# Two softmaxes by the tensor engine, and 18 identity products at the start

## The chip, the cores and the metric

The kernel runs on one core of a Trainium2 chip. The metric is device time in microseconds (us). The core has a tensor engine (PE; its weight loads are listed as PEld), a vector engine (DVE), a scalar engine (ACT), GpSimd (POOL) and a sync engine (SP), which here issues all loads and stores. Each engine works through its own queue in program order.

## The reference

Attention between 512 tokens and 32 state vectors, for 8 batches and 8 heads, then two layers of a network on all 4608 rows:

```python
scores = scale * np.matmul(x, state.transpose(0, 1, 3, 2))      # tokens x 32 states
a = softmax over the 32 states;   xread = np.matmul(a, state)
scores2 = scale * np.matmul(state, x.transpose(0, 1, 3, 2))     # 32 states x tokens
a2 = softmax over the 512 tokens; sread = np.matmul(a2, x)
x = concatenate([xread, sread], axis=2), heads side by side     # 4608 x 512
h = x @ w_in;  r = maximum(h, 0);  g = s * (r * r) + b;  x = g @ w_out      # 512 -> 2048 -> 512
h = maximum(x @ w_in2, 0);         out = h * h @ w_out2
```

Weights of the network come as doubles, which the kernel turns into single precision on the chip.

## The kernel before

A batch's scores are two tiles `sc` (r = 0 and 1, half of the heads each) of 128 partitions by 512 tokens: a partition is a head's state, four heads of 32 states stand below each other. So the softmax over states runs across groups of 32 partitions, and that over tokens along a row. `per_head` (L255) makes the scores with eight products into two PSUM tiles, and ScalarE copies them out (`att_sc`).

`att_exp` does both softmaxes' exponentials: the vector engine takes the maximum along the row (`nm2`), and it turns 32x32 blocks (`nc.vector.transpose`, L358) so that the other softmax too runs along the row: maximum of each 32, subtraction, exponential on ScalarE. `att_norm` sums, takes reciprocals and scales both. `att_an` turns the first softmax back and splits it into a high and a low part (`aT_t`), the moving operands of the first layer; `att_tp` turns the second by the tensor engine, and `att_sr` multiplies it with `xn` (x with tokens on the partitions); `att_put` copies the result into `sraw`.

The first layer goes in blocks of 128 hidden units: `mm1` (L448, tile `h`), `relu2` on ScalarE (three passes), `low` on the vector engine, and two blocks later `mm2` (L478, tile `acc`). Its weights `w_in` are multiplied with the state beforehand (`s_first` for batch 0, L288; `s_mm` for batch 1, L260), tile `S`. At the start the weights are still being loaded and converted: `piece` loads 128 columns or rows, `mag` is one ScalarE pass, `to_f32` four vector passes (L135 to L146). For the first blocks `early` does this between the products. The order of blocks is four of batch 0, four of batch 1, then the other twelve of each. The scheme is written out by hand: everything ahead of the loop stands in one sequence, and `at_step(i, fn, rank)` puts a piece of work behind block i, in the order of its rank. PSUM tiles rotate: four banks by `pst`, four by the pool `pa`, which also holds `acc`. Loads go out on SP's queue in program order, and one waits there when its buffer is not free (four buffers `raw` for weights, four `x` for `xT`, `xn` and `aT`).

Of the kernel before, what the change touches and what calls it, by code (L numbers as in the profile page):

```python
# [31 lines left out]
ALU = mybir.AluOpType  # L32
# [29 lines left out]
def attn_mlp2(ctx: ExitStack, tc: tile.TileContext, xT, xn, st, w_in1, w_out1, w_in2, w_out2, s_in, b_in, out):  # L62
# [40 lines left out]
    def x8(shape, name, dt=F32R):  # L103
        return xp.tile(shape, dt, tag="x", name=name)
# [225 lines left out]
            )  # L330
        xa[b] = [t, sb, None]

    def att_load_n(b):
        n = x8([P, S // P, DM], f"xn{b}", F32)
        nc.sync.dma_start(out=n, in_=xn[b].rearrange("(t p) d -> p t d", p=P))
        xa[b][2] = n

# [4 lines left out]
    def att_sc(b, _):  # L342
        t, sb, _ = xa[b]
        sps = [pst(f"sc{b}{r}") for r in range(2)]
        per_head(sps, sb, lambda rows, k: t[rows, k, :])
        for r, sp in enumerate(sps):
            sc = at.tile([P, S], F32, tag="sc", name="sc")
            nc.scalar.activation(out=sc, in_=sp, func=ACTF.Copy, scale=scale)
            cur[b, r] = [sc]

    def att_exp(b, c):
        (sc,) = cur[b, c]
# [36 lines left out]
    def att_tp(b, c):  # L389
# [4 lines left out]
        a2T = (at if b else op).tile([P, 4, P], F32, tag="t1" if b else "o", name="a2T")  # L394
        nc.scalar.copy(out=a2T, in_=tp.rearrange("p (a b) -> p a b", a=4))
        cur[b, c] = [a2T]

    def att_turn(b, c):
        att_an(b, c)
        att_tp(b, c)  # L400

    srp_t = {}

# [431 lines left out]
    def later(i, k, loader, rank=0):  # L835
# [12 lines left out]

    calm = ((att_sc, 0, 5), (att_exp, 0, 6), (att_exp, 1, 8), (att_norm, 0, 9), (att_norm, 1, 10),
            (att_an, 0, 11), (att_an, 1, 12), (att_tp, 0, 13), (att_tp, 1, 13), (att_sr, 0, 17), (att_put, 0, 17))  # L850
    first = ((att_exp, 0, 0), (att_exp, 1, 0), (att_norm, 0, 1), (att_norm, 1, 1), (att_turn, 0, 2),
             (att_turn, 1, 2), (att_sr, 0, 4), (att_put, 0, 4))
    rank = {att_sr: 0, att_tp: 0, att_sc: 0, att_put: 2, att_an: 3, att_turn: 3, att_exp: 5, att_norm: 5}
    for b in range(1, B):
        base = step(2, 0) + (b - 3) * NF if b > 1 else 0
        if b > 1:
            at_step(base + 1, lambda b=b: att_load(b), 6)
        at_step(base + 1, lambda b=b: att_load_n(b), 6)
        for fn, c, k in first if b == 1 else calm:
            at_step(base + k, lambda fn=fn, b=b, c=c: fn(b, c), rank[fn])  # L860
        for q in range(NQ):

# [144 lines left out]
    def finish(i):  # L1007
        for fn in lows.pop(i, []):
            fn()

    with tc.manual_schedule():
        make_identity(nc, ident)
        nc.scalar.activation(out=minus, in_=ident, func=ACTF.Copy, scale=-1.0)
        nc.gpsimd.memset(ones, 1.0)
        v0 = [piece("i1", w_in1, 0, 0)]
        att_load(0)
        v0 += [piece("i1", w_in1, 0, k) for k in range(1, VA)]
        nc.sync.dma_start(out=s_sb, in_=s_in.to_broadcast([P, 1]))
        nc.sync.dma_start(out=b_sb, in_=b_in.to_broadcast([P, 1]))
        v0[0]["mag"]()  # L1020
        to_f32(v0[0]["pair"]())
        att_sc(0, 0)
        s_first(0)
        att_exp(0, 0)
        s_first_lo(0)
        att_exp(0, 1)
        for p in v0[1:]:
            p["mag"]()
        att_load_n(0)
        att_load(1)  # L1030
        bring(0)
        bring(1)
        att_norm(0, 0)
        att_norm(0, 1)
        att_an(0, 0, lambda: to_f32(v0[1]["pair"]()))
        att_tp(0, 0)
        att_an(0, 1, lambda: to_f32(*[p["pair"]() for p in v0[2:]]))
        att_tp(0, 1)
        att_sc(1, 0)
        for p in stage[0]:  # L1040
            p["mag"]()
        at_step(1, lambda: att_sr(0, 0), 0)
        at_step(2, lambda: att_put(0, 0), 0)

        gs = {}
        for i in range(len(order) + LAG + 1):
# [57 lines left out]
```

## Time and profile before

| | us |
|---|---|
| three runs | 1406.64, 1407.17, 1409.31 (median 1407.17) |
| profiled execution: time, span | 1405.25, 1403.5 |
| PE busy, share of the span | 1371.6, 98% |
| PEld busy | 1159.5, 83% |
| DVE busy | 765.1, 55% |
| ACT busy | 759.1, 54% |

The span is the time between the first and the last instruction of the profiled execution; busy shares are means over stages that differ. In the profile's 40 equal slices of the span, PE is at 4 tenths in the first and at 9 in all others but the last.

### The profile page before, as it was taken

What the parts mean: (1) busy time and instruction counts of PE and PEld (TensorE: products, weight loads), DVE (VectorE), ACT (ScalarE), POOL (GpSimd) and SP (SyncE); (2) the same over time, 40 slices, a digit from 0 to 9 for tenths busy, and PEclk for the clock granted to TensorE, in tenths of its full rate; (3) what the DMA queues carried; (4) which work ended last, traced back from release to release, by engine and by line L of the source; (5) the groups of instructions that cost most, each with busy time, mean ns of one, the idle gap of its engine ahead of it and who ended that gap; (6) DMA issues with size and microseconds to landing.
All of it is one profiled execution on the core that took longest, in us unless ns stands there. A gap on an engine that the chain in (4) does not pass through costs nothing.

```text
span 1403.5 us, 20210 instructions
## 1 busy us (share of the span) xinstructions
PE 1371.6 (98%) x7770; PEld 1159.5 (83%) x7770; DVE 765.1 (55%) x1495; ACT 759.1 (54%) x1492; POOL 0.7 (0%) x7
## 2 busy tenths in 40 slices
PE   4999999999999999999999999999999999999998
PEld 2677777777777777889988999988999988999897
DVE  7888645555565767345667544453444435343533
ACT  4877656656665656557655543363344335434543
POOL 0000000000000000000000000000000000000000
PEclk9999999999999999999999999999999999999999
DMA  7365232332414241302663655445445544543652
GB/s 239 120 220 184 90 112 73 116 113 85 145 49 143 83 147 60 113 0 98 215 225 138 189 162 160 119 149 158 119 125 172 165 120 120 165 128 108 216 157 68
DMA packets 88863, 188.48 MB, mean 134 GB/s; under 512 B 8640, under 2 KB 26048, under 8 KB 86208
## 3 DMA queue, kind: packets, MB, share of 16 engines
q1 hardware_dynamic: 88768, 187.21, 42.5%
q8 instruction: 61, 1.00, 0.3%
q14 instruction: 34, 0.28, 0.1%
HBM read 144.18 MB, written 42.99 MB: 133 GB/s over the span
## 4 chain that ended last, share of the span: by engine, by line
PE 95%; DVE 3%; ACT 1%; DMA 0%; issue 0%; SPq 0%
PE o L681 27%; PE acc L478 26%; PE m L636 24%; PE h L448 14%; PE S L260 2%; PE sr L413 1%; PE sc L260 1%; PE tp L393 0%; PE S L288 0%; DMA xT<-xT 0%; DVE m L362 0%; DVE t L376 0%; DVE t L363 0%; DVE V L141 0%; DVE V L146 0%
## 5 line engine op out<-in xcount | busy, mean ns | idle before, releaser
L478 PE MATMUL acc<-g,o1h 128*128 128x512 f32 (+1 forms) x1152 | 341.2, 379 | 0.0
L478 PEld LDWEIGHTS acc<-g,o1h 128*128 128x128 f32 x1152 | 211.4, 188 | 41.7 <-issue 2.0
L478 PE MATMUL acc<-g,o1l 128*128 128x512 f32 (+1 forms) x576 | 217.5, 378 | 0.4 <-DVE o1l L189 0.4
L448 PE MATMUL h<-aT,S 128*128 128x512 f32 x768 | 201.9, 397 | 6.2 <-DVE aT L387 3.5
L448 PEld LDWEIGHTS h<-aT,S 128*128 128x128 f32 x768 | 141.4, 189 | 60.9 <-issue 9.2
L636 PE MATMUL m<-xw 128*128 128x384 f32 (+1 forms) x1008 | 183.4, 328 | 2.3 <-DVE r L715 2.3
L636 PEld LDWEIGHTS m<-xw 128*128 128x128 f32 x1008 | 171.5, 188 | 10.0 <-DVE r L715 2.6
L649 ACT ACTIVATE sc<-sc 128x384 f32<-128x384 f32 (+1 forms) x144 | 72.8, 505 | 153.2 <-DVE sc L715 151.7
L461 DVE TENSOR_TENSOR g<-r,g 128x512 fp32r<-128x512 f32 (+1 forms) x144 | 94.8, 658 | 111.0 <-ACT g L457 111.0
L455 ACT ACTIVATE r<-h 128x512 f32<-128x512 f32 (+1 forms) x144 | 82.2, 570 | 124.5 <-PE h L448 123.2
L649 ACT ACTIVATE v<-m 128x384 f32<-128x384 f32 (+1 forms) x96 | 45.5, 474 | 152.8 <-PE m L636 152.2
L478 PEld LDWEIGHTS acc<-g,o1l 128*128 128x128 f32 x576 | 108.4, 188 | 21.1 <-DVE o1l L189 0.9
L681 PE MATMUL o<-o2h,xw('g', 0)_6295 128*128 128x512 f32 x364 | 121.2, 392 | 0.0
L681 PE MATMUL o<-o2h,xw('g', 1)_6296 128*128 128x512 f32 x364 | 121.1, 392 | 0.0
L681 PE MATMUL o<-o2h,xw('g', 2)_6297 128*128 128x512 f32 x360 | 119.7, 392 | 0.0
L715 DVE TENSOR_TENSOR v<-m,r 128x384 f32<-128x384 f32 (+1 forms) x48 | 25.7, 536 | 164.4 <-PE m L636 164.4
L636 PE MATMUL m<-xw,xw('odd', 0)_6176 128*128 128x384 f32 (+1 forms) x576 | 107.4, 328 | 0.8 <-DVE t L715 0.8
L636 PEld LDWEIGHTS m<-xw,xw('odd', 0)_6176 128*128 128x128 f32 x576 | 98.3, 188 | 5.0 <-DVE t L715 1.2
L456 ACT ACTIVATE r<-r 128x512 f32<-128x512 f32 (+1 forms) x144 | 87.7, 609 | 4.6
L457 ACT ACTIVATE g<-r 128x512 fp32r<-128x512 f32 (+1 forms) x144 | 87.6, 609 | 4.6
L111 DVE TENSOR_TENSOR S<-S,S 128x512 fp32r<-128x512 f32 x54 | 34.8, 686 | 91.4 <-ACT S L110 91.4
L636 PE MATMUL m<-xw,xw('odd', 1)_6177 128*128 128x384 f32 (+1 forms) x432 | 79.3, 327 | 0.0
(146 smaller groups left out, 1893.5 us busy)
## 6 DMA issues: line engine op xcount, KB each, us to landing
xw<-w2s SPq DMA_DIRECT2D x140, 256.0 KB, 2.8
xw('odd', 0)_6176<-w2s SPq DMA_DIRECT2D x20, 1024.0 KB, 4.9
xw('odd', 1)_6177<-w2s SPq DMA_DIRECT2D x20, 768.0 KB, 4.3
i1r<-w_in SPq DMA_DIRECT2D x16, 512.0 KB, 5.0
xn<-xn SPq DMA_DIRECT2D x8, 1024.0 KB, 8.8
o1r<-w_out SPq DMA_DIRECT2D x16, 512.0 KB, 4.8
x<-ot SPq DMA_DIRECT2D x32, 256.0 KB, 3.0
i2r<-w_in SPq DMA_DIRECT2D x16, 512.0 KB, 5.3
```

Of the source, the lines that this page charges most:

```text
L111: nc.vector.tensor_tensor(out=lo, in0=src, in1=hi.bitcast(F32), op=ALU.subtract)
L260: nc.tensor.matmul(out=outs[r][k * NS : (k + 1) * NS], lhsT=state[rows, r, k, :], rhs=moving(rows, k), start=True, stop=True, skip_group_c ...
L448: nc.tensor.matmul(out=hp, lhsT=l_, rhs=r_, start=(i == 0), stop=(i == len(ops) - 1))
L455: nc.scalar.activation(out=r, in_=hp, func=ACTF.Relu)
L456: nc.scalar.activation(out=r, in_=r, func=ACTF.Square)
L457: nc.scalar.activation(out=g[:, 0], in_=r, func=ACTF.Copy)
L461: nc.vector.tensor_tensor(out=g[:, 1], in0=r, in1=g[:, 0].bitcast(F32), op=ALU.subtract)
L478: nc.tensor.matmul(out=o, lhsT=l_, rhs=r_, start=(opens and i == 0), stop=(closes and i == 2))
L636: nc.tensor.matmul(out=o, lhsT=w[:, a, k, :], rhs=x[:, b, k, :], start=(start and k + a + b == 0), stop=(k + a == 2), skip_group_check=True,)
L649: nc.scalar.activation(out=c, in_=src, func=func)
L681: nc.tensor.matmul(out=acc2[t], lhsT=l_, rhs=r_, start=(fa == 0 and e == 0), stop=(fa == NF - 1 and e == 2))
L715: add = lambda o, x, y: nc.vector.tensor_tensor(out=o, in0=x, in1=y, op=ALU.add)
```

## The change

For batches 0 and 1 the softmax over states no longer goes through the vector engine's block transposes. `soft_max` turns the scores with the tensor engine and takes the maximum of each 32 along the row from PSUM. `to_rows` brings these back to the layout of the scores: a product of a broadcast column with the identity, which adds minus the maximum onto the scores still lying in PSUM (`soft_exp`) or writes the reciprocals of the sums into another PSUM tile (`soft_norm`). `soft_sum` sums over each head's 32 partitions by products with `heads`, a matrix of ones and zeros. `soft_lo` makes the low part. The softmax over tokens is in `soft_state`; it stands behind blocks 0 and 3, and `att_tp`, `att_sr` and `att_put` follow later than before. `keep_on(18)` issues 18 products of the identity with itself ahead of everything else. The loads of batch 1 are issued ahead of `xn` of batch 0. The other batches stay as they are.

```diff
+    heads = const.tile([P, KD], F32, name="heads")
...
+    def soft_sc(b):
+        t, sb, _ = xa[b]
+        sps = [pa.tile([P, 512], F32, tag="acc", name=f"sc{b}{r}") if b else pst(f"sc{b}{r}") for r in range(2)]
+        per_head(sps, sb, lambda rows, k: t[rows, k, :])
+        for r, sp in enumerate(sps):
+            pool, tag = (at, "sc") if b else (op, "o")
+            sc = pool.tile([P, S], F32, tag=tag, name="sc")
+            nc.scalar.activation(out=sc, in_=sp, func=ACTF.Copy)
+            cur[b, r] = [sc]
+            cur["ps", b, r] = sp
+
+    def soft_max(b, r):
+        sc = cur[b, r][0]
+        tp = pa.tile([P, 512], F32, tag="acc", name=f"tm{b}{r}")
+        for i in range(4):
+            nc.tensor.transpose(out=tp[:, i * P : (i + 1) * P], in_=sc[:, i * P : (i + 1) * P], identity=ident)
+        m = cur["m", b, r] = sm.tile([P, 16, 1], F32, tag="m1", name="m1")
+        nc.vector.tensor_reduce(
+            out=m[:, :, 0], in_=tp.rearrange("p (a s) -> p a s", s=NS), axis=AX.X, op=ALU.max, negate=True
+        )
+
+    def to_rows(out, v, start):
+
+        for i in range(4):
+            for k in range(KD):
+                nc.tensor.matmul(
+                    out=out[k * NS : (k + 1) * NS, i * P : (i + 1) * P],
+                    lhsT=v[:, KD * i + k, :].to_broadcast([P, NS]),
+                    rhs=ident, start=start, stop=True, skip_group_check=True,
+                )
+
+    def soft_exp(b, r):
+        sp = cur.pop(("ps", b, r))
+        to_rows(sp, cur.pop(("m", b, r)), False)
+        e = cur["e", b, r] = at.tile([P, S], F32, tag="t1", name="e")
+        nc.scalar.activation(out=e, in_=sp, func=ACTF.Exp, scale=scale)
+
+    def soft_sum(b):
+        pt = pst(f"sum{b}")[:, : 32]
+        for r in range(2):
+            for i in range(4):
+                c0 = 16 * r + KD * i
+                nc.tensor.matmul(
+                    out=pt[:, c0 : c0 + KD], lhsT=cur["e", b, r][:, i * P : (i + 1) * P], rhs=heads,
+                    start=True, stop=True, skip_group_check=True,
+                )
+        for r in range(2):
+            s = cur["s", b, r] = sm.tile([P, 16, 1], F32, tag="s1", name="s1")
+            nc.vector.tensor_scalar(
+                out=s[:, :, 0], in0=pt[:, 16 * r : 16 * r + 16], scalar1=1e-9, scalar2=None, op0=ALU.add
+            )
+            nc.vector.reciprocal(out=s, in_=s)
+
+    def soft_norm(b, r):
+        pt = pst(f"inv{b}{r}") if b else pa.tile([P, 512], F32, tag="acc", name=f"inv{b}{r}")
+        to_rows(pt, cur.pop(("s", b, r)), True)
...
+        nc.vector.tensor_tensor(out=e, in0=e, in1=pt, op=ALU.mult)
+        nc.scalar.activation(out=aT_t[b][:, 0, r, :], in_=e, func=ACTF.Copy)
...
+    def soft_state(b, r):
+
+        (sc,) = cur[b, r]
+        nm2 = sm.tile([P, 1], F32, tag="nm2", name="nm2")
+        nc.vector.tensor_reduce(out=nm2, in_=sc, axis=AX.X, op=ALU.max, negate=True)
+        s2 = sm.tile([P, 1], F32, tag="s2", name="s2")
+        nc.vector.tensor_scalar(out=nm2, in0=nm2, scalar1=scale, scalar2=None, op0=ALU.mult)
+        nc.scalar.activation(out=sc, in_=sc, func=ACTF.Exp, bias=nm2, scale=scale, accum_out=s2)
+        nc.vector.tensor_scalar(out=s2, in0=s2, scalar1=1e-9, scalar2=None, op0=ALU.add)
+        nc.vector.reciprocal(out=s2, in_=s2)
+        nc.scalar.activation(out=sc, in_=sc, func=ACTF.Copy, scale=s2)
...
+    def keep_on(n):
+
+        pt = pa.tile([P, 512], F32, tag="acc", name="on")
+        for _ in range(n):
+            nc.tensor.matmul(out=pt[:, :P], lhsT=ident, rhs=ident, start=True, stop=True)
+
     with tc.manual_schedule():
         make_identity(nc, ident)
+        keep_on(18)
...
+        n0 = x8([P, S // P, DM], "xn0", F32)
+        att_load(1)
+        bring(0)
+        att_load_n(0, n0)
+        bring(1)
         v0[0]["mag"]()
         to_f32(v0[0]["pair"]())
-        att_sc(0, 0)
+        soft_sc(0)
+        soft_max(0, 0)
+        soft_max(0, 1)
         s_first(0)
-        att_exp(0, 0)
+        v0[1]["mag"]()
+        soft_exp(0, 0)
+        soft_exp(0, 1)
+        to_f32(v0[1]["pair"]())
+        v0[2]["mag"]()
+        soft_sum(0)
         s_first_lo(0)
-        att_exp(0, 1)
-        for p in v0[1:]:
-            p["mag"]()
-        att_load_n(0)
-        att_load(1)
-        bring(0)
-        bring(1)
-        att_norm(0, 0)
-        att_norm(0, 1)
-        att_an(0, 0, lambda: to_f32(v0[1]["pair"]()))
-        att_tp(0, 0)
-        att_an(0, 1, lambda: to_f32(*[p["pair"]() for p in v0[2:]]))
-        att_tp(0, 1)
-        att_sc(1, 0)
+        soft_norm(0, 0)
+        soft_norm(0, 1)
+        soft_lo(0, 0)
+        soft_lo(0, 1)
+        v0[3]["mag"]()
+        to_f32(*[p["pair"]() for p in v0[2:]])
+        soft_sc(1)
         for p in stage[0]:
             p["mag"]()
-        at_step(1, lambda: att_sr(0, 0), 0)
-        at_step(2, lambda: att_put(0, 0), 0)
+        for r in range(2):
+            at_step(0, lambda r=r: soft_max(1, r), -1)
+            at_step(0, lambda r=r: soft_state(0, r), 1)
+            at_step(1, lambda r=r: soft_exp(1, r), -1)
+            at_step(1, lambda r=r: att_tp(0, r), 0.5)
+            at_step(2, lambda r=r: soft_norm(1, r), -1)
+            at_step(2, lambda r=r: soft_lo(1, r), -1)
+            at_step(3, lambda r=r: soft_state(1, r), 1)
+            at_step(4, lambda r=r: att_tp(1, r), 1)
+        at_step(1, lambda: soft_sum(1), 0)
+        for b, i in ((0, 2), (1, 6)):
+            at_step(i, lambda b=b: att_sr(b, 0), 0)
+            at_step(i + 1, lambda b=b: att_put(b, 0), 0)
```

## Rows read from the trace of the kernel before

**Rows 1.** Busy us of PE, PEld, DVE, ACT, POOL; granted clock, DMA, GB/s.

```profile
20.00:25.00 5.00, 4.61 (x27) 2.28 (x27) 4.79 (x10) 1.65 (x3) 0.00 (x0) 1.00 0.18 71
25.00:30.00 5.00, 1.17 (x4) 0.47 (x3) 5.00 (x11) 2.65 (x5) 0.00 (x0) 0.72 0.46 124
30.00:35.00 5.00, 4.89 (x55) 3.33 (x54) 4.83 (x8) 2.02 (x5) 0.00 (x0) 0.59 1.00 338
35.00:40.00 5.00, 3.07 (x22) 1.86 (x20) 4.83 (x9) 4.97 (x13) 0.00 (x0) 0.75 0.46 174
40.00:45.00 5.00, 5.00 (x79) 3.78 (x78) 4.73 (x15) 4.94 (x10) 0.00 (x0) 0.91 0.36 105
70.00:80.00 10.00, 10.00 (x71) 7.49 (x70) 7.61 (x17) 7.43 (x16) 0.00 (x0) 1.00 0.63 197
```

**Rows 2.** What TensorE waited for after 100 us: total, times, longest.

```profile
PE m L636 <- DVE r L715: 2.3, 1, 2.3
```

**Rows 3.** Chain of waits, 12 to 49 us: start, us, what.

```profile
12.28 0.63 DVE t L358
...
25.34 0.64 DVE V L135 x2
...
29.06 0.60 DVE aT L387
...
48.28 0.21 DVE sraw L423
```

**Rows 4.** Products of TensorE in order of time: start, us, what, idle before.

```profile
20.07 1.94 PE L393 MATMUL tp<-ident,sc 128*128 128x128 f32 x8 [7.06 <-ACT sc L373]
...
21.94 1.96 PE L260 MATMUL sc<-xT,st 64*32 64x512 f32 x16
...
41.93 1.09 PE L260 MATMUL S<-V,st 64*32 64x512 f32 x16
...
48.63 1.06 PE L393 MATMUL tp<-ident,sc 128*128 128x128 f32 x8 [0.83 <-DVE sraw L423]
...
57.81 2.06 PE L413 MATMUL sr<-a2T,xn 128*64 128x32 f32 x64
...
61.39 0.64 PE L288 MATMUL S<-V,st 128*32 128x128 f32 x16
...
557.41 0.95 PE L231 MATMUL cs<-ones,wsum 128*128 128x2 f32 x8
```

**Rows 5.** Single instructions of the front, in order of time.

```profile
1.00 0.29 POOL masks.py:199 TENSOR_SCALAR_AFFINE_SELECT ident<-ident 128x128 f32<-128x128 f32 x1
...
8.98 0.20 PEld L260 LDWEIGHTS sc<-xT,st 64*32 64x32 f32 x8 [1.04 <-DMA xT<-xT]
...
23.83 0.50 PE L448 MATMUL h<-aT,S 128*128 128x512 f32 x1
...
34.00 0.59 ACT L455 ACTIVATE r<-h 128x512 f32<-128x512 f32 x1
...
40.13 0.59 ACT L455 ACTIVATE r<-h 128x512 f32<-128x512 f32 x1
...
44.44 0.39 PE L478 MATMUL acc<-g,o1h 128*128 128x512 f32 x1
...
65.63 1.55 PE L448 MATMUL h<-aT,S 128*128 128x512 f32 x6
```

**Rows 6.** Groups by line, 0 to 130 us: count, busy us, mean ns, idle before.

```profile
L382 DVE STREAM_TRANSPOSE an<-t 128x512 f32<-128x512 f32 x4 | 2.8, 707 | 0.1
...
L363 DVE TENSOR_TENSOR t<-t,m 128x512 f32<-128x512 f32 x4 | 2.8, 692 | 0.1
...
L372 DVE TENSOR_REDUCE s<-t 128x16 f32<-128x512 f32 x4 | 2.7, 666 | 0.0
...
L360 ACT ACTIVATE sc<-sc,nm 128x512 f32<-128x512 f32 x4 | 2.9, 724 | 1.0 <-DVE t L358 1.0
```

**Rows 7.** A wait of TensorE in the first 130 us: total, times, longest.

```profile
PE acc L478 <- DVE o1l L189: 0.4, 1, 0.4
```

More of the change, by code (lines that the diff above doesn't have):

```diff
@@ L331, in att_load, with att_load_n @@
         xa[b] = [t, sb, None]
-    def att_load_n(b):
-        n = x8([P, S // P, DM], f"xn{b}", F32)
+    def att_load_n(b, n=None):
+        n = x8([P, S // P, DM], f"xn{b}", F32) if n is None else n
         nc.sync.dma_start(out=n, in_=xn[b].rearrange("(t p) d -> p t d", p=P))
@@ new lines, in soft_norm, with soft_lo @@
+    def soft_norm(b, r):
+        pt = pst(f"inv{b}{r}") if b else pa.tile([P, 512], F32, tag="acc", name=f"inv{b}{r}")
+        to_rows(pt, cur.pop(("s", b, r)), True)
+        if r == 0:
+            aT_t[b] = x8([P, 2, 2, S], f"aT{b}")
+        e = cur["e", b, r]
+        nc.vector.tensor_tensor(out=e, in0=e, in1=pt, op=ALU.mult)
+        nc.scalar.activation(out=aT_t[b][:, 0, r, :], in_=e, func=ACTF.Copy)
+    def soft_lo(b, r):
+        hi, lo = aT_t[b][:, 0, r, :], aT_t[b][:, 1, r, :]
+        nc.vector.tensor_tensor(out=lo, in0=cur.pop(("e", b, r)), in1=hi.bitcast(F32), op=ALU.subtract)
@@ L396, in att_tp @@
         cur[b, c] = [a2T]
-    def att_turn(b, c):
-        att_an(b, c)
-        att_tp(b, c)
     srp_t = {}
@@ L850, in attn_mlp2 @@
             (att_an, 0, 11), (att_an, 1, 12), (att_tp, 0, 13), (att_tp, 1, 13), (att_sr, 0, 17), (att_put, 0, 17))
-    first = ((att_exp, 0, 0), (att_exp, 1, 0), (att_norm, 0, 1), (att_norm, 1, 1), (att_turn, 0, 2),
-             (att_turn, 1, 2), (att_sr, 0, 4), (att_put, 0, 4))
-    rank = {att_sr: 0, att_tp: 0, att_sc: 0, att_put: 2, att_an: 3, att_turn: 3, att_exp: 5, att_norm: 5}
+    rank = {att_sr: 0, att_tp: 0, att_sc: 0, att_put: 2, att_an: 3, att_exp: 5, att_norm: 5}
     for b in range(1, B):
@@ L858, in attn_mlp2 @@
         at_step(base + 1, lambda b=b: att_load_n(b), 6)
-        for fn, c, k in first if b == 1 else calm:
+        for fn, c, k in calm if b > 1 else ():
             at_step(base + k, lambda fn=fn, b=b, c=c: fn(b, c), rank[fn])
@@ L1009, in finish @@
             fn()
+    def keep_on(n):
+        pt = pa.tile([P, 512], F32, tag="acc", name="on")
+        for _ in range(n):
+            nc.tensor.matmul(out=pt[:, :P], lhsT=ident, rhs=ident, start=True, stop=True)
     with tc.manual_schedule():
         make_identity(nc, ident)
+        keep_on(18)
         nc.scalar.activation(out=minus, in_=ident, func=ACTF.Copy, scale=-1.0)
         nc.gpsimd.memset(ones, 1.0)
+        nc.gpsimd.memset(heads, 0.0)
+        for k in range(KD):
+            nc.gpsimd.memset(heads[k * NS : (k + 1) * NS, k : k + 1], 1.0)
         v0 = [piece("i1", w_in1, 0, 0)]
```

## The prediction

> **What bounds the kernel now.** I read the stretches by engine first, then the waits of TensorE, the chain of waits, and the instructions of the first 65 us in order of time. From 70 us the tensor engine has no idle time [rows 1], and after 100 us its longest wait for another engine is 2.3 us [rows 2]. So time can be won or lost only at the front, and every microsecond of tensor work that the front leaves undone is paid behind it. At the front the vector engine sets the pace: the chain stays on it from 12 us to the `sraw` copy at 48 [rows 3], and from 20 to 45 us it is busy at least 4.7 of every 5 us [rows 1]. The reader should see two more things in [rows 1]. ScalarE is just as full from 35 to 45 us (4.97 and 4.94 of 5). And the granted clock falls after the tensor engine idled 3.8 us in 25 to 30, and is below full again in 35 to 40, with 1.9 us idle.
>
> The column says 1.00 before 25 us, but I don't believe it there. Eight transposes take 1.94 us at 20 us and 1.06 at 48; sixteen instructions of 64x512 take 1.96 at 22 us and 1.09 at 42 [rows 4]. The early ones ran at about half. The Trainium skill (TensorE: Matmul & The Clock Gate, "What's actually happening") says that half rate is the default, which activity lifts. By the column alone the 18 identity products would buy nothing; by that page they buy what the next part counts. The durations side with the page.
>
> **The change, part by part.**
>
> *Identity products.* A full-precision product is two instructions (`per_head` issues eight products, the trace has 16). The nearest row has eight tiles of the array side by side, so 512 columns cost 0.55 us at full clock and 0.98 at half, and 128 columns 0.14 or 0.25 [rows 4]. 36 instructions: 4.9 to 8.8 us, an estimate. They can start at 1.3, when `ident` is written, and end at 6.2 to 10.1; the second half of `xT` releases the engine at 8.98 [rows 5]. I take about 8: hidden by that load. Without that cover they cost up to 1.1 us. In return the scores run at full clock, 0.9 us sooner at most.
>
> *First softmax of batch 0.* Removed for each of four (batch, half) pairs: two 32x32 transposes (L358 is the twin of L382), a subtraction and a sum, 2.8 us, so 11.1 us of vector time in all [rows 6]. Added on the tensor engine, by [rows 4]: four transposes 0.53; `to_rows`, 16 instructions of the shape of L288, 0.64, twice; `soft_sum`, 16 instructions a batch, for which the only row with a full stationary and few columns is L231, eight in 0.95, so 1.9. Bounds: L413 does 64 in 2.06, so 0.5 from below; half clock, 3.5, from above. L231 has the same stationary shape, so I take 1.9; `to_rows` has the same two bounds at 0.5 and 1.2. Reduction and product now read PSUM; with 0.67 and 0.69 from [rows 6] they stay where they are. From scores ready at about 9.7: copy 0.6, transposes 0.5, reduction 0.7, `to_rows` 0.6 twice, two exponentials 1.2, the second half of the sums 1.0, add and reciprocal 0.4 behind the conversion of a weight piece, `to_rows` 0.6, product 0.7, copy 0.6, and some 1.8 for handoffs and a magnitude pass. The first product of `h` starts at about 19, against 23.83 [rows 5]. The last two weight pieces (3.7 us of vector work, from 25.3 to 29.1, in [rows 3]) are converted by 23.4, and the first relu starts at 24.6 against 34.00 [rows 5]: a lead of 9.4 us.
>
> *Softmax of the state, moved behind.* `soft_state` is a strict relay: vector reduction and scale, scalar exponential (0.72 and its accumulator), vector add and reciprocal, scalar product. Both halves use both queues in that order, about 2.7 us each from [rows 6] with 0.2 for each small vector step, and the relu of block 1 is queued behind them on ScalarE. Block 1's relu is then at 32.5 against 40.13 [rows 5]: the lead is 7.6. `soft_exp` of batch 1 is queued behind that relu's three passes and two weight passes, five of about 0.6 us, so at 35.5. The tensor engine finished `to_rows` at 30 and stands in order before `soft_sum`: a gap of some 6 us that was not there.
>
> *The serial part.* After the gap come sums 1.9, transposes of `att_tp` 1.06, `s_mm` 1.09, block 2 of `h` 1.5 [rows 4, 5]: 5.5 us, and the first `acc` product at 41.5 against 44.44 [rows 5]. That is at full clock. Idle time of 3.8 us and even 1.9 went with half clock in [rows 1], so after 6 us I expect it, until about 41: these 5.5 us then cost 2.5 more, and `acc` starts at 44.0. The lead is gone.
>
> *Behind it.* From there to block 6 of `h` is 21.2 us before (44.44 to 65.63, [rows 5]). Added: two `to_rows`, 1.2. `att_sr` of batch 0 (2.06) comes in, that of batch 1 goes out to behind block 6. The waits of 0.8 for `sraw` [rows 4] and 0.4 for `o1l` [rows 7] go. New ones come: the vector queue stands behind the products with `to_rows`, then behind batch 1's state relay at 50 to 58 us, so the next two weight pieces are converted some 3.4 us later than now, and `s_first(4)`, the high and the low weights of block 3 each make the tensor engine wait: 0.6, 0.7 and 2.1 by the same arithmetic, 3.4 in all and 2.2 more than before. 44.0 + 21.2 + 1.2 + 2.2 = 68.6, 3.0 late; with the 2.06 of `att_sr` still undone, 5.0. If the clock returns some 2 us sooner, half of that loss goes and it is 4.0; if the clock never falls, 2.5. Loads moved ahead of `xn` on SP's queue cost nothing: `xn` of batch 0 is first read near 48 us, and `s_mm`'s inputs don't come by it.
>
> I take +4.0: in [rows 1] full clock is back within the stretch of 40 to 45, soon after the engine has work again. The profiled execution took 1405.25 us (span 1403.5), so 1409.25; the median of the three runs is 1.9 above it, and 4.0 on that is 1411.2.
>
> **The rivals.** What a measurement can tell from no change is about 0.2%, 2.8 us.
>
> *The clock holds* (same). The sum is +2.5, and with `soft_sum` at its lower bound +1.1: 1408.3 to 1409.7. For it: the identity products leave the engine at full clock, and its gaps in the first chain are short. Against it: the 6 us gap.
>
> *Vector and scalar engine stay ahead* (faster). The sum holds 9.4 us of new waits, 6 in the gap and 3.4 at blocks 3 to 5, all from two queues being in order. For it: 11.1 us less on the vector engine, which is what the chain ran on. Against it: ScalarE was full at 35 to 45 us and does as many passes as before. Without any of these waits and at full clock it is 2.5 - 9.4 = -6.9, 1400.3; from there on it is faster by more than 2.8 as long as they add up to under 4.1 us.
>
> *Half clock in the first chain too* (slower). If the engine falls back between its short pieces there, three `to_rows`, transposes and sums on the path cost up to 2 us more: 1412 to 1414. The skill's page speaks for it (same title, "HAM oscillation — how this bites in real kernels"): gaps between bursts throttle the array again. Against it: the identity products lift the clock first, and no wait inside the first chain of the sum is as long as the 1.9 us in [rows 1].
>
> *The front doesn't decide* (same). The lead of 9.4 us and the extra tensor work (eight `to_rows`, two sums, four transposes: 11 us, part of it in gaps) cancel: 1406 to 1408.
>
> **How the numbers follow.** Main case, +3 to +5.5: 0.40; half clock in the first chain too, up to +7: 0.10; clock holds: 0.23; cancels: 0.10; stays ahead: 0.17. So slower 0.50, same 0.33, faster 0.17. The predicted time is the main case's 1411.2, its own range 1409.8 to 1413. The range of 8 in 10 takes in both same cases, half of the faster one's reach, and the bounds of `to_rows` and sums: 1403.5 to 1414.
>
> **What would show it.** Right: `h` starts near 19 us; the relu of block 0 near 25; between `to_rows` and `soft_sum` of batch 1 a wait of TensorE for an exponential of ScalarE, 4 to 7 us, with a granted clock near 0.5 behind it; `acc` first at 43 to 45; the state relay on both engines at 50 to 58; waits for V, `o1h`, `o1l` near 60. Wrong: a gap under 2 us, or `acc` starting before 40, would make it faster; sums of `soft_sum` under 1 us would take off 1.3; identity products ending after 9 us would add to all of it. If after 100 us the waits differ from [rows 2], the argument that only the front counts is wrong.

## The result and the profile after

The changed kernel took 1415.07 us (median of 4 runs, 1414.16 to 1415.69) beside 1406.91 for the kernel before (4 runs, 1406.42 to 1409.31): a ratio of 1.0062, 95% interval 1.0048 to 1.0075. It is slower, by 8.2 us. The forecast had the sign; 1411.2 was 3.9 us short, and the time lies 1.1 us above the end of the range, 1414. The profiled executions are 1412.4 us of span against 1403.5, 8.9 apart.

In the changed kernel, L1090 are the identity products, L369 the transposes for the maximum, L379 `to_rows`, L389 the exponential of `soft_exp`, L396 `soft_sum`, L424 to L430 `soft_state`, L525 `h`, L532 the relu, L555 `acc`, L186 and L190 the high and low parts of a piece of `w_out`. First the stretches, with the columns of [rows 1].

```profile
20.00:25.00 5.00, 3.51 (x60) 2.38 (x57) 4.97 (x11) 2.63 (x7) 0.00 (x0) 1.00 0.53 181
25.00:30.00 5.00, 3.20 (x17) 2.02 (x16) 3.51 (x8) 4.68 (x11) 0.00 (x0) 0.92 0.98 320
30.00:35.00 5.00, 3.22 (x65) 2.76 (x64) 3.95 (x11) 4.22 (x8) 0.00 (x0) 0.74 0.53 194
35.00:40.00 5.00, 3.61 (x17) 3.62 (x18) 0.59 (x2) 1.82 (x4) 0.00 (x0) 0.60 0.35 105
40.00:45.00 5.00, 5.00 (x32) 3.02 (x32) 4.00 (x10) 2.30 (x5) 0.00 (x0) 0.71 0.11 22
...
60.00:65.00 5.00, 4.03 (x34) 2.65 (x32) 4.93 (x12) 4.36 (x9) 0.00 (x0) 1.00 0.21 58
65.00:70.00 5.00, 3.04 (x7) 2.46 (x8) 3.22 (x5) 3.95 (x8) 0.00 (x0) 0.68 0.55 195
70.00:80.00 10.00, 10.00 (x122) 7.73 (x125) 8.74 (x17) 4.44 (x9) 0.00 (x0) 0.99 0.78 246
```

The vector engine, 4.8 of every 5 us in [rows 1], is all but empty in 35 to 40 (0.59). Nothing fast took its place: TensorE too is idle 1.4 us of that stretch and runs the rest at 0.60. And there is a second hole, at 60 to 70, where [rows 7] had a wait of 0.4 us. What TensorE waited for in the first 130 us:

```profile
PE sum L396 <- ACT e L389: 3.2, 1, 3.2
PE acc L555 <- DVE o1l L190: 2.1, 1, 2.1
PE h L525 <- ACT S L307: 1.8, 1, 1.8
PE S L289 <- DVE V L147: 1.5, 1, 1.5
...
PE acc L555 <- ACT o1h L186: 0.5, 1, 0.5
PE S L289 <- ACT V L127: 0.3, 1, 0.3
```

The same engine in order of time (start, us, what, idle before):

```profile
1.36 6.16 PE L1090 MATMUL on<-ident 128*128 128x128 f32 x36 [1.36 <-POOL ident masks.py:199]
...
10.39 1.14 PE L369 MATMUL tm<-ident,sc 128*128 128x128 f32 x8 [0.70 <-ACT sc L361]
...
11.92 1.93 PE L379 MATMUL sc<-ident,m 128*32 128x128 f32 x64
13.79 1.94 PE L396 MATMUL sum<-heads,e 128*128 128x4 f32 x16
...
20.03 1.65 PE L525 MATMUL h<-aT,S 128*128 128x512 f32 x6
...
30.01 3.21 PE L379 MATMUL sc<-ident,m 128*32 128x128 f32 x64
36.39 3.57 PE L396 MATMUL sum<-heads,e 128*128 128x4 f32 x16 [3.17 <-ACT e L389]
39.82 1.95 PE L474 MATMUL tp<-ident,sc 128*128 128x128 f32 x8
...
44.76 0.62 PE L555 MATMUL acc<-g,o1h 128*128 128x512 f32 x2
...
48.04 1.95 PE L379 MATMUL inv<-ident,s 128*32 128x128 f32 x64
49.92 2.06 PE L490 MATMUL sr<-a2T,xn 128*64 128x32 f32 x64
...
66.96 0.80 PE L555 MATMUL acc<-g,o1l 128*128 128x512 f32 x1 [2.06 <-DVE o1l L190]
...
70.97 1.56 PE L525 MATMUL h<-aT,S 128*128 128x512 f32 x6
...
564.79 0.95 PE L232 MATMUL cs<-ones,wsum 128*128 128x2 f32 x8
```

ScalarE's side of the hole at 33 to 36 us: the state softmaxes of batch 0 (one row of each half), then the relu of block 1, then the exponentials that the sums wait for.

```profile
25.25 0.59 ACT L532 ACTIVATE r<-h 128x512 f32<-128x512 f32 x1
...
28.93 0.73 ACT L427 ACTIVATE sc<-sc,nm 128x512 f32<-128x512 f32 x1
...
32.24 0.72 ACT L430 ACTIVATE sc<-sc,s 128x512 f32<-128x512 f32 x1 [0.48 <-DVE s L429]
32.87 0.58 ACT L532 ACTIVATE r<-h 128x512 f32<-128x512 f32 x1
...
35.75 1.07 ACT L389 ACTIVATE e<-sc 128x512 f32<-128x512 f32 x2
```

How the lead is lost can be read off against [rows 5]. The relu of block 0 is 8.75 us sooner (25.25 for 34.00), that of block 1 7.26 (32.87 for 40.13). The first `acc` is 0.32 late (44.76 for 44.44), block 6 of `h` 5.34 late (70.97 for 65.63), and the column sums near the end of the first layer 7.38 late (564.79 against [rows 4]). The other 1.5 of the 8.9 us come in the second layer.

### The profile page after: what moved, and what is told of

Same layout as the page of the kernel before. It is cut to its first block, busy times and chain, and to the rows that moved or that the text cites. A ratio compares the mean times of both kernels' runs of the same rounds, so it can differ in the third digit from the quotient of the medians.

```text
span 1412.4 us, 20884 instructions
## 1 busy us (share of the span) xinstructions
PE 1391.3 (99%) x8110; PEld 1179.9 (84%) x8110; DVE 755.0 (53%) x1483; ACT 760.1 (54%) x1492; POOL 1.2 (0%) x12
## 4 chain that ended last, share of the span: by engine, by line
PE 96%; ACT 2%; DVE 1%; DMA 0%; issue 0%; SPq 0%; ACTq 0%; DVEq 0%
PE o L758 26%; PE acc L555 26%; PE m L713 23%; PE h L525 14%; PE S L261 2%; PE sr L490 1%; PE S L289 1%; PE sc L261 1%; PE tp L474 0%; DMA xT<-xT 0%; PE sum L396 0%; PE inv L379 0%; ACT sc L427 0%; DVE V L142 0%; ACT sc L430 0%
## 5 line engine op out<-in xcount | busy, mean ns | idle before, releaser
L555 PE MATMUL acc<-g,o1h 128*128 128x512 f32 (+1 forms) x1152 | 342.0, 380 | 0.5 <-ACT o1h L186 0.5
L555 PEld LDWEIGHTS acc<-g,o1h 128*128 128x128 f32 x1152 | 212.1, 189 | 42.5 <-issue 2.0
L555 PE MATMUL acc<-g,o1l 128*128 128x512 f32 (+1 forms) x576 | 218.3, 379 | 2.1 <-DVE o1l L190 2.1
L525 PE MATMUL h<-aT,S 128*128 128x512 f32 x768 | 200.1, 396 | 1.8 <-ACT S L307 1.8
L525 PEld LDWEIGHTS h<-aT,S 128*128 128x128 f32 x768 | 140.9, 188 | 55.0 <-issue 9.2
L532 ACT ACTIVATE r<-h 128x512 f32<-128x512 f32 (+1 forms) x144 | 82.2, 571 | 126.3 <-PE h L525 126.3
L555 PEld LDWEIGHTS acc<-g,o1l 128*128 128x128 f32 x576 | 108.8, 189 | 23.0 <-DVE o1l L190 2.5
L758 PE MATMUL o<-o2h,xw('g', 0)_6474 128*128 128x512 f32 x364 | 121.2, 392 | 0.0
L758 PE MATMUL o<-o2h,xw('g', 1)_6475 128*128 128x512 f32 x364 | 121.1, 392 | 0.0
L758 PE MATMUL o<-o2h,xw('g', 2)_6476 128*128 128x512 f32 x360 | 120.3, 394 | 0.0
L713 PE MATMUL m<-xw,xw('odd', 0)_6355 128*128 128x384 f32 (+1 forms) x576 | 107.4, 328 | 0.8 <-DVE t L792 0.8
L713 PEld LDWEIGHTS m<-xw,xw('odd', 0)_6355 128*128 128x128 f32 x576 | 98.3, 188 | 5.0 <-DVE t L792 1.2
L713 PE MATMUL m<-xw,xw('odd', 1)_6356 128*128 128x384 f32 (+1 forms) x432 | 79.3, 327 | 0.0
```

The source lines that it names most:

```text
L525: nc.tensor.matmul(out=hp, lhsT=l_, rhs=r_, start=(i == 0), stop=(i == len(ops) - 1))
L532: nc.scalar.activation(out=r, in_=hp, func=ACTF.Relu)
L555: nc.tensor.matmul(out=o, lhsT=l_, rhs=r_, start=(opens and i == 0), stop=(closes and i == 2))
L713: nc.tensor.matmul(out=o, lhsT=w[:, a, k, :], rhs=x[:, b, k, :], start=(start and k + a + b == 0), stop=(k + a == 2), skip_group_check=True,)
L758: nc.tensor.matmul(out=acc2[t], lhsT=l_, rhs=r_, start=(fa == 0 and e == 0), stop=(fa == NF - 1 and e == 2))
```

## The experiments

The runs were made in four groups, and the kernel before ran beside each, on the chip of that group: 1406.0, 1406.1, 1406.38 and 1406.71 us. Ratios are to those, and differences between groups are taken from the ratios.

### The clock and the identity products

**Filling the holes.** The change with 31 more identity products.

```diff
+        at_step(0, lambda: keep_on(7), 2)
+        at_step(1, lambda: keep_on(16), -0.5)
...
+            if i == 5:
+                keep_on(8, True)
```

> The changed kernel with 31 more identity products in three gaps: 7 behind block 0, 16 behind the to_rows of batch 1 (where the tensor engine waits 3.2 us), 8 ahead of block 3's acc (where it waits 2.1 us). Clock theory: the half clock from 36 to 42.4 us and from 67 to 70 us, which follows these gaps, costs 2.5 and 1.6 us; it goes, and the time falls from 1415 to 1410 to 1412. Work theory (the tensor engine's extra instructions are simply paid): the fillers add work, 1415 to 1418.

1410.3 us, ratio 1.0031 (1.0020 to 1.0042): 4.3 us above the kernel before in place of 8.2, so 3.9 come back. Its stretches:

```profile
30.00:35.00 5.00, 5.00 (x91) 4.50 (x90) 3.94 (x11) 4.19 (x8) 0.00 (x0) 1.00 0.69 242
35.00:40.00 5.00, 4.60 (x50) 3.65 (x48) 2.03 (x9) 2.93 (x6) 0.00 (x0) 0.96 0.33 105
40.00:45.00 5.00, 5.00 (x26) 3.38 (x15) 2.58 (x4) 2.51 (x5) 0.00 (x0) 0.70 0.36 110
65.00:70.00 5.00, 5.00 (x38) 3.74 (x36) 4.38 (x9) 3.40 (x7) 0.00 (x0) 1.00 0.69 238
720.00:740.00 20.00, 20.00 (x101) 17.97 (x100) 14.69 (x32) 11.84 (x26) 0.00 (x0) 1.00 0.74 250
```

The clock is at 1.00, 0.96 and 1.00 at 30 to 35, 35 to 40 and 65 to 70, where the change had 0.74, 0.60 and 0.68; one fall, at 40 to 45, is left. The products compute nothing and take tensor time, so what they gave back is the price of the clock (its lower level, 0.50 in the rows, is 1.2 GHz). In the traces 2.4 us of it stand at the end of the first layer (column sums at 562.44 for 564.79). The other 1.5 come from a fall in the second layer that the traced execution of the change has and this one has not (below); no filler stands there. Most of the other 4.3 us is something else.

**Without the 18 identity products.**

```diff
-        keep_on(18)
```

> The changed kernel without the 18 identity products. Clock theory: the first chain runs at half clock, h starts 1 to 2 us later than 20.0, and as the same queues follow, the end is 1 to 2 us later: 1416 to 1417. Rival: the lead is lost in the later gap anyway, so nothing changes, 1414.5 to 1415.5. Second rival: the products delay the scores, 1414.

1418.48 us, ratio 1.0085 (1.0069 to 1.0100), more than was expected. Its first chain:

```profile
11.51 1.94 PE L369 MATMUL tm<-ident,sc 128*128 128x128 f32 x8 [0.79 <-ACT sc L361]
...
14.23 3.16 PE L379 MATMUL sc<-ident,m 128*32 128x128 f32 x64
...
24.33 1.84 PE L525 MATMUL h<-aT,S 128*128 128x512 f32 x6
```

The transposes take 1.94 us for 1.14, `to_rows` 3.16 for 1.93, and `h` starts at 24.33 for 20.03. The column of the granted clock reads 1.00 in this run too until 20 us; the durations decide. So without them the chain runs at half clock, which was a rival of the prediction, and they are worth more than the 0.9 us that the prediction allowed them: the ratios differ by 0.23%, 3.2 us.

**The kernel before with the 18 identity products alone.**

> The kernel before with the 18 identity products alone. Its front runs on the vector engine from 11.6 us on, which starts when the scores are copied. If only the scores are sooner, by at most 0.9 us, the time falls by 0.5 to 1: 1406. Rival: with the clock up from the start, transposes and scores of batch 1 at 20 to 24 us run at full clock too, but they are not on the vector engine's chain: nothing more, and if the products end late, no gain: 1407.

1404.78 us, ratio 0.9990 (0.9981 to 0.9999): 1.2 us less, a little more than was expected. This is the fastest complete kernel of the study, so it is what the rest of the change has to beat: against it the changed kernel loses 10.1 us (by the ratios). The relu of block 0 comes at 30.58 and that of block 1 at 36.71, 3.4 us sooner than in [rows 5]; the first `acc` comes at 43.94, only 0.5 sooner.

**The kernel before with 64 identity products** (18 in front, 36 behind the first cut of S, 10 at the end of step 0).

> The kernel before with the 18 identity products (as run alone: 0.999 of before) and 46 more: 36 behind the first cut of S, where TensorE waits 7.2 us for the first softmax, and 10 at the end of step 0. Clock theory: the granted clock stays at 1.00 from 10 to 40 us in place of 0.50 to 0.85, the first acc comes 1 to 2 us sooner, 1402 to 1404.5 us. Rival (VectorE sets the first 40 us, 4.7 to 4.9 busy of every 5, and a faster TensorE only waits longer): 1404 to 1406 us, as without them.

1405.64 us, ratio 0.9994 (0.9986 to 1.0003): nothing beyond the first 18. In its trace the clock is 1.00 from 10 to 25 and from 35 to 45 us, where 18 alone left 0.80, 0.50, 0.50, 0.50 and 0.62. The first `acc` starts at 41.15, and then TensorE waits 2.8 us at 47 for the `sraw` copy on VectorE; block 6 of `h` is at 65.89 (65.63 in [rows 5]). The faster tensor engine only waits longer there, as VectorE has 4.6 to 4.9 us of work in every 5 from 10 to 45, and behind that wait the clock falls (0.83 from 45 to 55).

### The parts of the change

**No state softmax** in batches 0 and 1 (`soft_state` does nothing, so this part of the result is left out; the rest of the change stays).

> The changed kernel without the softmax over tokens of batches 0 and 1 (soft_state does nothing: a2 stays the scores; that part of the result is left out). Queue theory: the relay of soft_state on the vector and scalar engine is what holds the relu of block 1, the exponentials of batch 1 and the weight pieces at 60 us; without it the gap before soft_sum and the waits near 65 us close, the clock stays up, and the time falls by 5 to 7: 1408 to 1410. Work theory: the tensor engine does the same work, so it falls by 0 to 2: 1413 to 1415.

1404.65 us, ratio 0.9989 (0.9980 to 0.9998). The four relays, in the change 2.9 to 3.9 us each from the reduction to the end of the last product, come out, and 10.3 us with them (by the ratios), more than was expected. What TensorE then waits for, 0 to 130 us:

```profile
PE sum L396 <- ACT e L389: 0.3, 1, 0.3
```

The wait of the sums falls from 3.2 to 0.3, and those for `o1h` and `o1l` near 65 us are gone: there `o1l` is cut at 60.0 us. It also bounds what a better place for the relays can bring: with its state softmaxes free, the change would gain 1.4 us on the kernel before, and that is what the 18 identity products give alone (1404.78). The two softmaxes on TensorE have nothing over the old way even then.

**Batch 0 the new way, batch 1 as before.**

```diff
-        for fn, c, k in calm if b > 1 else ():
+        for fn, c, k in calm if b > 1 else first:
...
-        soft_sc(1)
+        att_sc(1, 0)
...
+            at_step(0, lambda r=r: soft_state(0, r), 1)
+            at_step(1, lambda r=r: att_tp(0, r), 0.5)
```

> Batch 0 goes the changed way (maximum and sum by transposes and products, state softmax at step 0, identity products in front); batch 1 goes as before, with its softmaxes on VectorE and ScalarE at steps 0 to 2 and its sr at step 4. Main theory (the loss is in the waits of the serial chain of batch 1, soft_exp(1) to h, behind the state softmax, and in the half clock that its idle time brings): batch 1's chain is off TensorE, but VectorE gets back some 11 us of maximum, exponentials and products that sit before the first block of batch 1; the first relu stays at about 25, first acc at 43 to 46; 1408 to 1412 us. Rival (VectorE's work of the first 45 us decides, wherever it stands): batch 1 the old way puts that work back in front of the relus, so 1413 to 1417 us, no better than the whole change.

1407.85 us, ratio 1.0008 (1.0000 to 1.0017), at the lower end of the main theory. Relu of block 0 at 26.42, of block 1 at 39.19, first `acc` at 45.43: 6.2 us behind relu 1. Beside the kernel before with the 18 products, the first relu is 4.2 us sooner, the second 2.5 later and the time 2.5 above it (by the ratios): the lead is gone at the next relu.

**Batch 1 the new way, batch 0 as before.**

```diff
-        soft_sc(0)
-        soft_max(0, 0)
-        soft_max(0, 1)
+        att_sc(0, 0)
...
-            at_step(0, lambda r=r: soft_state(0, r), 1)
```

> Batch 0 goes as before (all its softmaxes on VectorE and ScalarE ahead of the first h), batch 1 the changed way, with the changed order of loads and the identity products kept. Main theory: first h at about 24, relu of block 0 at 30 to 33, no state softmax of batch 0 behind it at step 0, so soft_exp(1) is not held back and its chain runs while h of batch 0 keeps TensorE busy; first acc at 43 to 45, block 6 of h at 66 to 68; 1407 to 1411 us, between before and the change. Rival (the products to rows on TensorE and the half clock are the loss by themselves): 1412 to 1415 us.

1417.15 us, ratio 1.0075 (1.0063 to 1.0088): a miss, by more than the rival too. With no state softmax between the relus, relu 1 still comes at 37.20 and the first `acc` at 50.25. The distance between these two tells where batch 1's new way is dear: 13.0 us here, 11.9 in the change, and 4.3 in the kernel before [rows 5]. Sums, transposes (here `sr` of batch 0, 3.31 us), S and `h` follow each other on TensorE behind an exponential that comes after the relu, with the clock at 0.81 and 0.51 from 40 to 50. Batch 0's new way gains up to the first relu, batch 1's spends it. The time of this run is not the price of the serial part alone: batch 1's relays still stand ahead of block 3, with the change's wait of 2.06 us for `o1l` and a clock of 0.54 behind it (70 to 75). So my reading that only the relay ahead of exp(1) costs was too narrow; the serial part, which the prediction had priced, costs with or without it.

### The place of the state softmaxes

**Later: batch 0 at steps 3 and 4, batch 1 at 8 and 9.**

```diff
-            at_step(0, lambda r=r: soft_state(0, r), 1)
+            at_step(3 + r, lambda r=r: soft_state(0, r), 7)
...
-            at_step(1, lambda r=r: att_tp(0, r), 0.5)
+            at_step(5, lambda r=r: att_tp(0, r), 0.5)
...
-            at_step(3, lambda r=r: soft_state(1, r), 1)
-            at_step(4, lambda r=r: att_tp(1, r), 1)
+            at_step(8 + r, lambda r=r: soft_state(1, r), 7)
+            at_step(10, lambda r=r: att_tp(1, r), 1)
...
-        for b, i in ((0, 2), (1, 6)):
+        for b, i in ((0, 7), (1, 12)):
```

> The whole change, but the state softmaxes stand later: those of batch 0 at steps 3 and 4 behind everything else (before: step 0), its transposes at step 5, sr at 7; those of batch 1 at steps 8 and 9, transposes at 10, sr at 12. No work is left out. Main theory (what costs is that the state softmax of batch 0, 5.8 us on VectorE and ScalarE in a row, stands between the relu of block 0 and that of block 1 and ahead of exp(1)): the time is that of the change without it (1404.7) plus 0 to 2 for the work in a fuller place, 1404 to 1408 us. Rival (the amount of the work counts, not its place): 1412 to 1415 us, as the change.

1415.58 us, ratio 1.0062 (1.0049 to 1.0075): no gain at all, half a microsecond above the rival's range. The trace, and the run with the relays in the gaps below, speak for the place and not the amount. The first `acc` is 3.2 us sooner, at 41.58, and TensorE comes to the first `o1l` of block 3 at 59.3 us, 5.6 sooner than in the change, also because the transposes and `sr` of both batches now stand behind it. There it waits 2.0 us longer than in the change:

```profile
58.56 0.73 PE L555 MATMUL acc<-g,o1h 128*128 128x512 f32 x2 [0.53 <-ACT o1h L186]
63.35 0.76 PE L555 MATMUL acc<-g,o1l 128*128 128x512 f32 x1 [4.07 <-DVE o1l L190]
```

VectorE, just ahead of it: between the last pass over the piece of `w_out` (`v`) and the low part `o1l` that TensorE waits for stand the second half's state softmax and the four passes (L136 to L147) over the next piece of `w_in`.

```profile
57.16 0.68 DVE L147 SCALAR_TENSOR_TENSOR v<-o1r,v 128x512 uint32<-128x512 uint32 x1
...
58.36 0.68 DVE L424 TENSOR_REDUCE nm<-sc 128x1 f32<-128x512 f32 x1
...
60.30 0.17 DVE L429 RECIPROCAL s<-s 128x1 f32<-128x1 f32 x1
60.38 0.41 DVE L136 TENSOR_SCALAR V<-V 128x512 f32<-128x512 f32 x1
...
62.62 0.68 DVE L190 TENSOR_TENSOR o1l<-v,o1h 128x512 fp32r<-128x512 f32 x1
```

There is a gate, then, in this kernel: the cut of the piece of `w_out` for block 3, whose low part starts at 60.0 us without any state softmax. TensorE passes it 3.6 us sooner than in the change (63.35 for 66.96), but with two pairs of transposes and two `sr` still to do, 6.2 us, where the change has one `sr`, 2.1. What was moved from ahead of the wait to behind it made the wait longer and is paid all the same.

**The same with 23 fillers** in the holes at 27 to 36 us.

> As the one with the later state softmaxes, and 23 more identity products (7 at the end of step 0, 16 in step 1 ahead of the sum) to fill the idle time of TensorE between 27 and 36 us. Clock theory: the granted clock stays 1.00 to 45 us, first acc at 40 to 41.5, and the time is 1 to 3 us below the one without them: 1402 to 1406 us. Rival (without the state softmax there is no idle time to fill, the products only delay the sum): equal or 1 to 2 us above it.

1413.71 us, ratio 1.0053 (1.0040 to 1.0067). The clock is at 1.00 from 25 to 60 and the first `acc` at 40.76. The wait for `o1l` is as long as before, but it ends 1.5 us sooner:

```profile
61.86 0.80 PE L555 MATMUL acc<-g,o1l 128*128 128x512 f32 x1 [4.06 <-DVE o1l L190]
```

So the gate has no fixed time; it moves with the front. The median is 1.9 us below the one without them, a gain as the clock theory had it, at a level that neither theory gave; the two intervals overlap, so the gain is not clear of the noise.

**In the gaps:** batch 0's behind exp(1) in step 1, batch 1's at the end of step 6.

```diff
-            at_step(0, lambda r=r: soft_state(0, r), 1)
+            at_step(1, lambda r=r: soft_state(0, r), -0.5)
...
-            at_step(1, lambda r=r: att_tp(0, r), 0.5)
+            at_step(2, lambda r=r: att_tp(0, r), 0.5)
...
-            at_step(3, lambda r=r: soft_state(1, r), 1)
-            at_step(4, lambda r=r: att_tp(1, r), 1)
+            at_step(6, lambda r=r: soft_state(1, r), 7)
+            at_step(8, lambda r=r: att_tp(1, r), 1)
...
-        for b, i in ((0, 2), (1, 6)):
+        for b, i in ((0, 3), (1, 10)):
```

> The whole change, with the four state softmaxes put where the trace of the change shows VectorE and ScalarE idle together: those of batch 0 in step 1 behind exp(1) (35 to 40 us there: VectorE 0.59, ScalarE 1.82 of 5), those of batch 1 at the end of step 6 (VectorE waits for loads there); transposes at 2 and 8, sr at 3 and 10. Theory now (some 2 us of every state softmax on VectorE count where the cutting of w_out for the first products of block 3 is late, and nowhere else; moving them to steps 3 and 4 left that place as full as it was): no wait of acc for o1l near 60 us, first acc at 41 to 43, block 6 of h at 62 to 65, 1404 to 1408 us. Rival (the work costs the same in any place of the first 100 us): 1412 to 1416 us again.

1407.74 us, ratio 1.0008 (0.9999 to 1.0016). The same work in another place costs 7.6 us less (by the ratios), and the wait for `o1l` is 0.2. One new wait shows behind it, for a cut piece of `w_in`:

```profile
82.66 1.12 PE L289 MATMUL S<-V,st 128*32 128x128 f32 x32 [1.83 <-DVE V L136]
```

Batch 1's relays now stand on VectorE at 67.6 to 72.0, and from there to 84 it works without a gap of 0.2 us. That speaks for its queue, and not the loads, as the cause of this wait.

**The same with 22 fillers.**

> The one with the state softmaxes in the gaps, and 22 identity products (10 at the end of step 0, 12 in step 1 ahead of the sum). If the clock still falls at 35 to 42 us without them, they give back up to 2.5 us: 1402 to 1406 us, first acc at 40 to 41.5. Rival: the cutting of w_out for block 3 is what sets the time at 60 us, and an earlier first acc only waits there: equal within 1 us to the one without.

1409.25 us, ratio 1.0018 (1.0009 to 1.0027). The first `acc` comes at 40.17 for 41.11, block 6 of `h` at 62.19 for 63.14, and the traced executions differ by the same 0.9 us (1406.80 for 1407.74). But this one is the fastest of its ten, and the median is not better. The ten stand in the order of their mean granted clock: 1406.8 us at 0.999, 1407.9 to 1408.4 at 0.998, 1409.2 to 1409.9 at 0.997 and 1411.8 to 1412.2 at 0.995. The fillers do not hold the clock in every execution.

**The relays in the gaps, with `sr` of batch 1 ahead of the new wait** (transposes at 7, `sr` at 8).

> The one with the state softmaxes in the gaps, with one thing more: the transposes and sr of batch 1 at steps 7 and 8 (there 8 and 10). There TensorE waits 3.7 us for cut weights at 82 to 87 us and runs sr (2.06 us) after that wait; here sr runs ahead of it and comes out of the wait: block 11 of h 1.5 to 2 us sooner, 1405 to 1406.5 us. Rival (the wait is for loads that start when TensorE has come so far, so it moves with sr): 1407 to 1409 us, no change.

1408.46 us, ratio 1.0011 (1.0003 to 1.0020): by the time, the rival. The 3.7 us of waiting that the expectation starts from are not there: 1.8 stand at 81 to 82.7, and the other 1.9, a wait for `V`, end at 25.6 us. In this run a wait of 1.1 us for ScalarE at 77 is left, but the time stayed.

**Only batch 1's moved** (end of step 6).

> The change with only the two state softmaxes of batch 1 moved (step 3 to the end of step 6, transposes 8, sr 10); those of batch 0 stay at step 0. It parts the two places. If each place costs by its own wait: the wait of 2.06 us for o1l and the fall of the clock behind it (1.6 us) go, the late first chain stays: first acc at 44.8 as in the change, block 6 of h at 66 to 68, 1410 to 1412 us. Rival (only the work ahead of the first acc counts): 1414 to 1416 us.

1413.43 us, ratio 1.0047 (1.0035 to 1.0059). Between the two theories. The wait for `o1l` falls from 2.1 to 0.7 us and the clock behind it stays at 1.00 (65 to 70); the first `acc` is at 46.48, even later, since half clock lasts through the stretch of 40 to 45.

**Only batch 0's moved** (step 1, behind exp(1); transposes 2, `sr` 3).

> The change with only the two state softmaxes of batch 0 moved (step 0 to step 1 behind exp(1), transposes at 2, sr at 3); those of batch 1 stay at step 3. If the two places lie in series, the first acc comes at 41 to 42, 3 us sooner than in the change, and the cutting of w_out for block 3, late by the softmaxes of batch 1, takes it back: a wait of acc for o1l of 4 to 5 us near 60 us in place of 2.06, and 1411 to 1414.5 us. Rival (the gains of the two places add up): 1415.1 less the 5.7 that the other move left, 1409 to 1410 us.

1407.32 us, ratio 1.0007 (0.9997 to 1.0016): better than either theory. All but the whole loss comes from the place of one batch's two relays, and moving the other batch's too gives no more (1.0008 above). Its waits:

```profile
PE sum L396 <- ACT e L389: 1.7, 1, 1.7
PE acc L555 <- DVE o1l L190: 1.5, 1, 1.5
```

Relu 1 comes at 31.22 (32.87 in the change), the exponentials at 34.12 (35.75), the first `acc` at 42.28 (44.76), `o1l` lets TensorE go at 64.55 (66.96), and block 6 of `h` is at 67.07 (70.97). So 1.6 us at the relu grow to 2.5, with the clock back sooner (0.78 for 0.71 at 40 to 45 us). They reach the gate as 2.4, and there the wait of 1.5 leaves the clock at 1.00 (65 to 70 us) where the change's 2.1 went with 0.68. That is 3.9 us, and 3.9 is also the difference of the two profiled executions (1410.29 and 1414.16). But this one is the highest of its 11 times (1406.15 to 1410.29), and the change's the lowest of its 4. The other 3 to 4 us go with the clock: four executions with a mean granted clock of 0.996 took 1406.2 to 1406.7 us, five at 0.995 took 1407.1 to 1410.3, two at 0.994 took 1409.9. At that same 0.994 the change took 1414.2 and 1414.6, so 4.3 to 4.8 us part the two kernels there; its other two, at 0.992 and 0.993, took 1415.5 and 1415.7. Which falls of the clock the faster executions lack, no trace here shows.

## Why the prediction fell short, step by step

The mechanism was right: the lead, the gap at the sums, half clock behind the gap, waits near 60 us. Sizes failed, and each is a price of the clock on TensorE: the discount of 1.0 for an early return of full clock, which did not come, and two falls of the clock that the sum put at nothing, 1.5 us behind the wait for `o1l` and 1.5 in the second layer. A smaller term was `to_rows`, counted at two thirds of its price at full clock.

**What bounds it.** Right. From 70 us TensorE is busy throughout, the longest wait after 100 us is 2.3 us as in [rows 2], and what the front lost stayed lost.

**Identity products.** 6.16 us, inside the estimate of 4.9 to 8.8, ended at 7.5 and hidden by `xT`, whose second half came at 8.62. Their return was mis-sized: 0.9 at most was allowed, for the scores alone; they kept the whole first chain at full clock, 3.2 us. The sum itself had the chain at full clock, so this did not move the forecast. The Trainium skill (TensorE: Matmul & The Clock Gate, "What's actually happening") has half rate as the default; the run without them agrees, with transposes of 1.94 us for 1.14.

**First softmax and first chain.** `h` at 20.03 (19 forecast), relu 0 at 25.25 (24.6). `soft_sum` took 1.94 (1.9). `to_rows` took half as much again as counted: the trace has two instructions for each of the 16 products of a call, 32 in all, as the prediction itself says of `per_head`. A pair of calls took 1.93 us at full clock and 3.21 at half, where 1.28 was counted.

**State relay and exp(1).** Relu 1 at 32.87 (32.5), exp(1) at 35.75 (35.5). The gap was 3.2 us and not 6, because TensorE finished `to_rows` at 33.2 instead of 30, by its half clock and a wait of 1.8 for S. That changed nothing: the sums start at 36.39 by the exponentials. The start was right, and the length of the gap was not.

**Serial part.** At half clock until about 42, forecast until about 41 (sums 3.57 us for 1.94, transposes 1.95 for 1.06; `h` at 43.26 is back at 1.66): 8.4 us from sums to `acc` (8.0 forecast), `acc` at 44.76 (44.0).

**Behind it: here it failed, in size.** From `acc` to block 6 of `h` 24.6 us were forecast and 26.2 came. The waits were as described, at V, `o1h` and `o1l`, 0.3, 0.5 and 2.1 (0.6, 0.7, 2.1). `to_rows` took 0.75 more. And the clock fell a second time behind the wait for `o1l`, which the sum didn't have: from `o1l` to `h` 4.0 us, against 2.5 in the run with batch 0's relays moved. The `sr` still undone was right (2.06). So 5.0 at this point became 7.4.

**The clock's return.** The sum took 1.0 off for a return some 2 us before 41. It didn't come: the transposes at 39.82 still took 1.95. It had rested on one row, the 0.91 of the stretch from 40 to 45 in [rows 1], where TensorE had other work behind it.

**After 100 us.** The waits don't differ, as forecast, but the clock does. Behind the same wait of 2.25 us in the second layer it stayed at 1.00 in the kernel before and fell in the changed one (the products behind the wait, then start:end, span and the rest as above):

```profile
721.80 2.03 PE L713 MATMUL m<-xw 128*128 128x384 f32 x6 [2.25 <-DVE r L792]
...
721.00:723.00 2.00, 1.20 (x5) 1.20 (x6) 2.00 (x6) 1.08 (x3) 0.00 (x0) 0.78 0.76 247
723.00:725.00 2.00, 2.00 (x7) 1.71 (x7) 0.36 (x2) 1.10 (x3) 0.00 (x0) 0.50 0.92 336
```

The same wait in the kernel before:

```profile
714.43 1.33 PE L636 MATMUL m<-xw 128*128 128x384 f32 x6 [2.25 <-DVE r L715]
...
710.00:715.00 5.00, 2.75 (x14) 2.22 (x13) 3.75 (x8) 2.59 (x6) 0.00 (x0) 1.00 0.29 79
715.00:720.00 5.00, 5.00 (x27) 4.57 (x26) 2.71 (x6) 2.99 (x6) 0.00 (x0) 1.00 0.52 186
```

From this wait to the next group of twelve `m` products it is 5.0 us for 3.5. That is the last 1.5 us: 4.0 forecast, 1.0 for the discount, 0.8 to the first `acc`, 1.6 behind it, 1.5 here, 8.9 in all.

**The rivals.** "Stays ahead" needed the waits to add up to under 4.1 us; those at the sums, V, `o1h` and `o1l` are 6.1 (3.2, 0.3, 0.5, 2.1), and the last brought a second fall of the clock. The nearest to it is the run without state softmaxes: 1404.65, not 1400.3, with the clock at 0.66 to 0.90 from 30 to 45. "Half clock in the first chain" is what the identity products prevented. "The clock holds" was tried with fillers: 1410.3, not 1408.3 to 1409.7, with one fall at 40 to 45 us left. "The front doesn't decide" fails on the runs that change the front alone: 1404.65 to 1418.48.

**What stays open.** Executions of one kernel differ by 4 us (the one with batch 0's relays moved), and with it about half of what that move gave. This goes with their mean granted clock, but as one execution of each kernel was traced, neither the places of the falls nor what sets them off is shown.

## What to carry to other kernels

A moved step is priced by what stands behind it in both queues that it uses: two short relays put in front of a relu cost 7.7 of the 8.2 us (by the ratios), and one step later, behind the exponential, nearly nothing. Look for the next gate behind a gain (here a cut weight piece at 60 us): tensor work moved from ahead of it to behind it is paid there, and the wait grows. Take a change apart before it is judged: its 18 identity products alone made the kernel before faster, and the rest only cost. A new wait of TensorE needs a second line in the sum, with a chance, for the clock behind it, and a price per call is the count of instructions in the trace, not of products in the source.

## What the runs showed of the hardware that was not expected

The same wait of 2.25 us of TensorE, in the same code of the second layer, stands in all sixteen traces. In four the clock fell behind it, and the six products there took 1.78 to 2.21 us; in twelve they took 1.31 to 1.33. At 65 us a wait of 2.1 with 0.5 before it went with 0.68, one of 1.5 with 1.00. Idle time of this length is thus no sure sign of a fall.

Products that compute nothing bought 3.9 us in the changed kernel. In the kernel before, 46 of them beyond the first 18 bought nothing. They lifted the clock in both (mean of the profiled executions 0.994 to 0.998, and 0.990 to 0.996). The same shows without fillers: in the runs with the relays in the gaps a lower mean clock goes with a longer time, while of the kernel before, beside two of them, 15 executions at 0.990 took 1405.4 to 1408.0 us and four at 0.994 took 1406.5 to 1407.0.
